# Attention, routed experts and a bilinear network in one kernel: bias constants built first on GpSimd, the mask folded into the distance, and idle products on TensorE

## The chip, the cores and the metric

The kernel runs on one core of a Trainium2 chip. The metric is the device time of one execution in microseconds (us). The two kernels differ in a few small instructions, in their order, and in products whose result nobody reads; the output is the same array.

## What is computed

Three stages follow each other. Attention over q, k, v of shape (4, 8, 576, 64), in a causal window of 128 with a slope per head on the distance:

```python
rel = pos[:, None] - pos[None, :]
slopes = 2.0 ** (-8.0 * (np.arange(H) + 1) / H)
mask = (rel >= 0) & (rel < 128)
scores = np.where(mask, scale * q @ k.T + slopes * -np.abs(rel), -1e9)
x = softmax(scores) @ v                      # then 2304 tokens of 512
e = argmax(x @ w_gate + modality_bias[modality_id])      # one of 8 experts
x = prob[e] * (relu(x @ w1[e]) @ w2[e])      # 512 -> 1024 -> 512
out = ((x @ m_w1) * (x @ m_w2)) @ m_w3 @ m_wout          # m_*: 64-bit weights
```

## The kernel before, in words

Large products are made of three products of two-part numbers (a high part and a rest): `mm3` at L290 to L292, and six half-height products per pair of heads in `scores` at L387. `split` (L273 on ScalarE, L275 or L277 on VectorE) makes the two parts. In the first nine chunks `split_pe` lets TensorE subtract the high part with a scaled identity, `id_k` or `id_q` (L283, L284, L287).

**Attention.** Queries come in chunks of 128 per batch (four and a tail of 64). A unit is a chunk and a half of its heads, 40 units in all. A unit passes through `scores` (TensorE), `softmax` (VectorE adds `bias` to the scores and takes the minimum, L415; ScalarE does the exponential, L420), `p_transposes` (L440) one unit later and `attend` (L459) two units later. Scores are negated, so the mask is a large positive bias. The transposes of the next chunk (L307) and its loads (L166, on the SyncE queue) stand between the units. Also between them, from unit 5 on, the 64-bit weights are loaded (`raw_wo`, `raw_w`, L697) and turned into 32-bit numbers on VectorE (`to_f32`, L710 to L723), and `m_w3 @ m_wout` is built up in the PSUM tile `pw` of tag "G".

**Constants.** `build_constants` makes on GpSimd the identity (L187, L188), the distance `rel` and a separate mask `msk` (L195 to L203: an iota, a cast, a memset, four selections), then on VectorE `bias` of 8 heads as distance times slope plus mask (L209), and after that the smaller constants: `ones_b`, `tri_b`, the zeros of `qz` (L221). `build_constants2` (called at unit 2: gate weights, ten small loads, `mid_f`, and L254 to L266 on VectorE) and `build_constants3` (at unit 3) follow.

**Experts.** Tokens are gathered by expert in blocks of 480 (`gather_x`, L980), transposed in four parts of 120 (`block_transposes`, L1001), and run through `ffn_step`: products `ph` and `py`. Five blocks are in the program in any case. At the **border** to the last network the outputs go through memory: `ys` is written, `load_y` reads it (L1183), `x2_split` makes its two parts, `w_late` (L1133) has eight leftover products on TensorE, and then `ab_step` (products `p`) and `out_step` (products `po`) run to the end.

**Order.** Each engine runs its own list in order. The lists are laid out ahead of time from the program's order and from simulated times; `with tc.issue_after(x)` keeps the instructions of the block behind x in the list of x's engine, and does no more than that. SyncE issues nearly all loads in one list.

Of the kernel before, what the change touches and what calls it, by code (L numbers as in the profile page):

```python
# [18 lines left out]
P = 128  # L19
# [29 lines left out]
def kernel(  # L49
# [134 lines left out]
    def build_constants():  # L184
        scr = a_p.tile([P, 3, 2 * P], F32, tag="p", name="scr", bufs=2)
        rel_i, rel, msk = scr[:, 0, :].bitcast(I32), scr[:, 1, :], scr[:, 2, :]
        nc.gpsimd.memset(ident, 0.0)  # L187
        nc.gpsimd.affine_select(  # L188
            out=ident, in_=ident, pattern=[[-1, P]], compare_op=ALU.not_equal, fill=1.0,
            base=0, channel_multiplier=1,  # L190
        )
        for t, f in ((id_k, -1.0), (id_q, 1.0 / SCALE)):
            nc.vector.tensor_scalar_mul(t, ident, f)

        nc.gpsimd.iota(rel_i, pattern=[[-1, 2 * P]], base=P, channel_multiplier=1)  # L195
        nc.gpsimd.tensor_copy(rel, rel_i)
        nc.gpsimd.memset(msk, 0.0)
        for t, fill in ((rel, 0.0), (msk, MASK)):
            nc.gpsimd.affine_select(
                out=t, in_=t, pattern=[[-1, 2 * P]], compare_op=ALU.is_ge, fill=fill,  # L200
                base=P, channel_multiplier=1,
            )
            nc.gpsimd.affine_select(  # L203
                out=t, in_=t, pattern=[[1, 2 * P]], compare_op=ALU.is_ge, fill=fill,
                base=-1, channel_multiplier=-1,
            )
        for h in range(H):
            slope = 2.0 ** (-8.0 * (h + 1) / H)
            nc.vector.scalar_tensor_tensor(  # L209
                out=bias[:, h, :], in0=rel, scalar=slope, in1=msk, op0=ALU.mult, op1=ALU.add  # L210
            )
# [12 lines left out]
        nc.gpsimd.tensor_copy(iota_em, ie)  # L224
# [44 lines left out]
    last = {}  # L269

    def split(hi, lo, src, scale=1.0):

# [8 lines left out]
    def split_pe(hi, lo, tp, scale=1.0):  # L281

        nc.scalar.activation(out=hi, in_=tp, func=AF.Copy, scale=scale)  # L283
        nc.tensor.matmul(  # L284
            tp, lhsT=id_q if scale != 1.0 else id_k, rhs=hi, start=False, stop=True, skip_group_check=True,
# [3 lines left out]
    def mm3(dst, lh, ll, rh, rl, start, stop):  # L289
        nc.tensor.matmul(dst, lhsT=lh, rhs=rh, start=start, stop=False)  # L290
        nc.tensor.matmul(dst, lhsT=lh, rhs=rl, start=False, stop=False)  # L291
        return nc.tensor.matmul(dst, lhsT=ll, rhs=rh, start=False, stop=stop)  # L292

# [10 lines left out]
    def head_transposes(nm, b, c, tp, hps):  # L304
        t = raw[nm, b, c]
        for hp in hps:
            nc.tensor.matmul(  # L307
                tp[:, hp, :],
# [64 lines left out]
    def scores(b, c, hq):  # L373
# [6 lines left out]
        for t in range(2):  # L380
            hp = 2 * hq + t
            if c < NF:
                for i, (l, r) in enumerate(((ql, kh), (qh, kl), (qh, kh))):

                    for j in (1, 0):
                        d = slice(j * D, (j + 1) * D)
                        last["s"] = nc.tensor.matmul(  # L387
                            s[j][:, t, :nk], lhsT=l[d, hp, :], rhs=r[d, hp, ks],
# [43 lines left out]
    def p_transposes(b, c, hq):  # L432
# [3 lines left out]
        for j in range(2 if c < NF else 1):  # L436
            pt = pst("P", [P, 2, 2, P], f"PT_{b}_{c}_{hq}_{j}")
            for t in range(2):
                for kb in range(nkb):
                    nc.tensor.transpose(pt[:, t, kb, :], p[:, j, t, kb * P : (kb + 1) * P], ident)  # L440
            nc.scalar.copy(pT[:, j, :, :nkb, :], pt[:, :, :nkb, :])  # L441
        st_T[b, c, hq] = pT

    def attend(b, c, hq):
# [6 lines left out]
        for t in range(2):  # L451
            hp = 2 * hq + t
            for i, (kb, cc) in enumerate(kbs):
                for j in (1, 0):
                    if c < NF:
                        pj = pT[:, j, t, kb, :]
                    else:
                        pj = pT[:, 0, t, kb, j * TAIL : (j + 1) * TAIL]
                    nc.tensor.matmul(  # L459
                        av[j * D : (j + 1) * D, hp, : P if c < NF else TAIL],  # L460
# [26 lines left out]
    def gate_logits(i, g, pos):  # L487
# [5 lines left out]
        for d in range(ND):  # L493
            nc.tensor.transpose(
                tp[:, 2 * d : 2 * d + 2, :].rearrange("p h d -> p (h d)"), xt[:, d, :], ident
            )
        lp = pst("A", [P, H, E], f"lg_{i}")
        if i in rs:

            r = rs.pop(i)  # L500
            for d in range(ND):
                nc.tensor.matmul(
                    lp[:, 2 * d : 2 * d + 2, :], lhsT=xt[:, d, :], rhs=wgb[:, d, :, :],
# [13 lines left out]
        else:  # L517
            for d in range(ND):
                nc.tensor.matmul(
                    lp[:, 0, :], lhsT=xt[:, d, :], rhs=wg[:, d, :],  # L520
# [9 lines left out]
    def route(g, i0, m):  # L530
# [30 lines left out]
        for j in range(i0, i0 + m):  # L561
# [3 lines left out]
        rk = pst("A", [P, 6, E], f"rk_{g}")  # L565
        nc.tensor.matmul(
            rk[:, :m, :], lhsT=tri_b, rhs=hot_b[:, sl, :], start=True, stop=False
        )
        nc.tensor.matmul(
            rk[:, :m, :], lhsT=ones_b, rhs=hcum[:, sl, :], start=False, stop=True  # L570
# [21 lines left out]
    def block_table():  # L592
# [6 lines left out]
        np_ = pst("A", [P, 6, E], "cnt")  # L599
        nc.tensor.matmul(np_[:, 0, :], lhsT=ones_b, rhs=hcum[:, NT, :], start=True, stop=True)  # L600

# [151 lines left out]
    def w3_transposes(i, sp=split):  # L753
# [4 lines left out]
        for j in range(4):  # L758
            nc.tensor.matmul(
                tp[:, j, :], lhsT=x[:, j * P : (j + 1) * P], rhs=ident, is_transpose=True,  # L760
# [79 lines left out]
    load_chunk(*chunks[1], "v")  # L840
    extras = {2: [build_constants2], 3: [build_constants3], 5: [fill_rest]}
# [151 lines left out]
    def block_transposes(b, u):  # L993
# [6 lines left out]
        for d in range(ND):  # L1000
            nc.tensor.transpose(tp[:, d, :RU], xb[b][u][:RU, d * P : (d + 1) * P], ident[:RU, :RU])  # L1001
        us = slice(u * RU, (u + 1) * RU)
# [126 lines left out]
    def w_late(f, k):  # L1129

        tag, bufs = (("S", 2), ("P", 2), ("G", 1), ("V", 1), ("S", 2), ("P", 2))[k % 6]
        late[f] = pst(tag, [P, DM], f"pl_{f}", bufs=bufs)
        nc.tensor.matmul(late[f], lhsT=w3_last[:, f, :], rhs=wo_last, start=True, stop=True)  # L1133

# [116 lines left out]
    for f in range(LATE, NMC):  # L1251
        w_late(f, f - LATE + 2)
    for h in range(M_PRE):
        split_m(h)
# [66 lines left out]
```

## Time and profile before

| | us |
|---|---|
| runs of the kernel before | 793.8, 801.9, 802.56 |
| median | 801.9 |
| the profiled execution | 802.81 |
| its span, first to last instruction | 801.1 |
| around the span | 1.7 |
| TensorE busy | 761.4 (95%) |
| VectorE busy | 392.7 (49%) |
| ScalarE busy | 326.6 (41%) |
| GpSimd busy | 70.1 (9%) |

The span holds attention up to about 245 us, the experts up to about 485 us and the last network from 495 us on. TensorE's busy time is modelled and covers all of the pipelined products, so 95% does not say that it runs at its best rate. The mean granted clock of TensorE is 0.979 of full speed.

### The profile page before, as it was taken

What the parts mean: (1) busy time and instruction counts of PE and PEld (TensorE: products, weight loads), DVE (VectorE), ACT (ScalarE), POOL (GpSimd) and SP (SyncE); (2) the same over time, 40 slices, a digit from 0 to 9 for tenths busy, and PEclk for the clock granted to TensorE, in tenths of its full rate; (3) what the DMA queues carried; (4) which work ended last, traced back from release to release, by engine and by line L of the source; (5) the groups of instructions that cost most, each with busy time, mean ns of one, the idle gap of its engine ahead of it and who ended that gap; (6) DMA issues with size and microseconds to landing.
All of it is one profiled execution on the core that took longest, in us unless ns stands there. A gap on an engine that the chain in (4) does not pass through costs nothing. (4 is left out here: it accounts for less than half of the span.)

```text
span 801.1 us, 11805 instructions
## 1 busy us (share of the span) xinstructions
PE 761.4 (95%) x4363; PEld 631.6 (79%) x4363; DVE 392.7 (49%) x1045; ACT 326.6 (41%) x757; POOL 70.1 (9%) x113
## 2 busy tenths in 40 slices
PE   7788999998998899999999997999999999999996
PEld 5676777786776788888888884888888888888895
DVE  4799678685655466566667515541122123023020
ACT  5788677675553334343424313442222122122121
POOL 4000201001013200010100000001000000100101
PEclk9999999998999999999999998999999999999999
DMA  7677645453102958484745204002002000100100
GB/s 154 204 212 204 155 120 148 117 145 81 53 28 68 284 169 265 136 249 138 220 160 165 79 1 130 29 0 79 27 0 79 27 1 27 53 1 0 40 14 27
DMA packets 100502, 81.92 MB, mean 102 GB/s; under 512 B 69850, under 2 KB 83418, under 8 KB 100437
## 3 DMA queue, kind: packets, MB, share of 16 engines
q1 hardware_dynamic: 93925, 66.52, 29.5%
q0 software_dynamic: 3632, 9.66, 3.6%
q10 hardware_dynamic: 2880, 4.92, 1.6%
q8 instruction: 36, 0.59, 0.3%
q14 instruction: 29, 0.24, 0.1%
HBM read 66.36 MB, written 14.54 MB: 101 GB/s over the span
## 5 line engine op out<-in xcount | busy, mean ns | idle before, releaser
L1214 DVE TENSOR_TENSOR a<-a,p 128x512 f32<-128x512 f32 (+1 forms) x40 | 25.4, 634 | 189.7 <-PE p L292 183.5
L275 DVE TENSOR_TENSOR fwl<-fw,fwh 128x1024 fp32r<-128x1024 f32 x40 | 49.0, 1225 | 77.3 <-ACT fwh L273 75.7
L273 ACT ACTIVATE fwh<-fw 128x1024 fp32r<-128x1024 f32 x40 | 42.4, 1061 | 92.4 <-PE ph L291 66.9
L420 ACT ACTIVATE p<-p,mn 128x256 f32<-128x256 f32 (+2 forms) x144 | 68.0, 476 | 27.1 <-DVE mn L415 25.4
L290 PE MATMUL ph<-xbh,fwh 128*128 128x480 f32 x160 | 62.1, 389 | 0.7 <-ACT xbh L273 0.7
L290 PE MATMUL p<-x2h,m0h 128*128 128x512 f32 (+1 forms) x160 | 59.5, 372 | 3.2 <-ACT x2h L273 3.2
L292 PE MATMUL ph<-xbh,fwl 128*128 128x480 f32 x160 | 61.4, 384 | 0.0
L291 PE MATMUL ph<-xbl,fwh 128*128 128x480 f32 x160 | 61.2, 382 | 0.0
L291 PE MATMUL py<-hl,fwh 128*128 128x480 f32 x160 | 60.4, 381 | 0.0
L290 PE MATMUL p<-x2h,m1h 128*128 128x512 f32 (+1 forms) x160 | 59.4, 374 | 0.0
L291 PE MATMUL p<-x2l,m1h 128*128 128x512 f32 (+1 forms) x160 | 59.3, 371 | 0.0
L292 PE MATMUL p<-x2h,m1l 128*128 128x512 f32 (+1 forms) x160 | 59.3, 371 | 0.0
L291 PE MATMUL p<-x2l,m0h 128*128 128x512 f32 (+1 forms) x160 | 59.1, 369 | 0.0
L292 PE MATMUL p<-x2h,m0l 128*128 128x512 f32 (+1 forms) x160 | 59.1, 369 | 0.0
L273 ACT ACTIVATE abh<-a 128x512 fp32r<-128x512 f32 (+1 forms) x40 | 23.5, 588 | 84.6 <-DVE a L1214 84.6
L292 PE MATMUL py<-hh,fwl 128*128 128x480 f32 x160 | 57.9, 380 | 0.0
L290 PE MATMUL py<-hh,fwh 128*128 128x480 f32 x160 | 57.6, 379 | 0.0
L291 PE MATMUL po<-Wl,abh 128*128 128x512 f32 (+1 forms) x152 | 57.3, 378 | 0.0
L290 PE MATMUL po<-Wh,abh 128*128 128x512 f32 (+1 forms) x152 | 57.3, 378 | 0.0
L292 PE MATMUL po<-Wh,abl 128*128 128x512 f32 (+1 forms) x152 | 56.8, 378 | 0.0
L415 DVE CUSTOM_DVE_ANT_0 p<-S,bias 128x256 f32<-128x256 f32 (+1 forms) x128 | 43.4, 386 | 15.5 <-PE S L387 8.9
L459 PE MATMUL av<-pT,vr 128*64 128x128 f32 (+1 forms) x576 | 45.2, 275 | 1.4 <-ACT pT L441 1.1
(231 smaller groups left out, 1616.8 us busy)
## 6 DMA issues: line engine op xcount, KB each, us to landing
fw<-in_moe_w_dram SPq DMA_DIRECT2D x40, 512.0 KB, 4.2
raw_w<-in_moe_w_dram SPq DMA_DIRECT2D x16, 512.0 KB, 4.2
raw_m<-in_moe_w_dram SPq DMA_DIRECT2D x16, 512.0 KB, 3.7
ys_dram<-y ACTq DMA_DIRECT2D x20, 240.0 KB, 4.5
vr<-in_v_dram SPq DMA_DIRECT2D x16, 256.0 KB, 3.7
raw_wo<-in_moe_w_out_dram SPq DMA_DIRECT2D x8, 512.0 KB
xs_dram<-x SPq DMA_DIRECT2D x16, 256.0 KB
yt<-ys_dram SPq DMA_DIRECT2D x8, 512.0 KB, 4.3
```

The costliest lines, as they stand in the source:

```text
L273: last["a"] = nc.scalar.activation(out=hi, in_=src, func=AF.Copy, scale=scale)
L275: last["v"] = nc.vector.tensor_tensor(out=lo, in0=src, in1=f32(hi), op=ALU.subtract)
L290: nc.tensor.matmul(dst, lhsT=lh, rhs=rh, start=start, stop=False)
L291: nc.tensor.matmul(dst, lhsT=lh, rhs=rl, start=False, stop=False)
L292: return nc.tensor.matmul(dst, lhsT=ll, rhs=rh, start=False, stop=stop)
L415: nc.vector.tensor_tensor_reduce(out=p[:, j, t, :nk], in0=s[j][:, t, :nk], in1=bi, scale=1.0, scalar=BIG, op0=ALU.add, op1=ALU.min, accum_ ...
L420: nc.scalar.activation(out=p[:, j, t, :nk], in_=p[:, j, t, :nk], func=AF.Exp, scale=-1.0, bias=m1, accum_out=sm[:, col : col + 1],)
L459: nc.tensor.matmul(av[j * D : (j + 1) * D, hp, : P if c < NF else TAIL], lhsT=raw["v", b, cc][:, 2 * hp + j, :], rhs=pj, start=(i == 0), s ...
L1214: nc.vector.tensor_tensor(out=a[:, :nt], in0=a[:, :nt], in1=pp[1][:, :nt], op=ALU.mult)
```

## The change

In `build_constants` the order on GpSimd becomes identity, iota, cast, two selections, and nothing else. The selections write a far distance, 1e9 times 2^8, outside of the window, so that every head's slope (2^-1 to 2^-8) leaves at least 1e9 there; the mask's memset, its two selections and the tile `msk` go. `bias` is then one scaled copy per head (`tensor_scalar_mul`) instead of `scalar_tensor_tensor` with two inputs. The memset of `ones_b` goes to VectorE, ahead of everything. The rest of the constants (`build_constants1`, and the GpSimd part of `build_constants2` and `3`) stays behind the last of the two selections (`p_mark`) in GpSimd's list.

Idle products, `ones_b` by `ones_b` of 128x512 in bfloat16 into a PSUM tile that nobody reads, are added on TensorE: 5 before the first load has landed, 1 behind the first transposes, 2 behind the scores of each of the units 0 to 4, 2 behind the second half of chunk 0's transposes, 2 behind the transposes of chunks 1 and 2 (22 in the head); 3 behind each of the four parts of the first block's transposes (12); and 16 at the border behind the last of the `w_late` products. Except for the first 5 they are kept behind the TensorE instruction that the program issued last.

```diff
 def build_constants():
-    nc.gpsimd.memset(msk, 0.0)
-    for t, fill in ((rel, 0.0), (msk, MASK)):
-        nc.gpsimd.affine_select(out=t, in_=t, pattern=[[-1, 2 * P]], compare_op=ALU.is_ge, fill=fill,
-            base=P, channel_multiplier=1)
-        nc.gpsimd.affine_select(out=t, in_=t, pattern=[[1, 2 * P]], compare_op=ALU.is_ge, fill=fill,
-            base=-1, channel_multiplier=-1)
+    nc.vector.memset(ones_b, 1.0)
+    far = MASK * 2.0**8
+    nc.gpsimd.affine_select(out=rel, in_=rel, pattern=[[-1, 2 * P]],
+        compare_op=ALU.is_ge, fill=far, base=P, channel_multiplier=1)
+    mark = nc.gpsimd.affine_select(out=rel, in_=rel, pattern=[[1, 2 * P]],
+        compare_op=ALU.is_ge, fill=far, base=-1, channel_multiplier=-1)
     for h in range(H):
-        nc.vector.scalar_tensor_tensor(
-            out=bias[:, h, :], in0=rel, scalar=slope, in1=msk, op0=ALU.mult, op1=ALU.add)
-    nc.gpsimd.memset(ones_b, 1.0)
+        nc.vector.tensor_scalar_mul(bias[:, h, :], rel, 2.0 ** (-8.0 * (h + 1) / H))
+    return mark
+
+def build_constants1():
     nc.gpsimd.memset(tri_b, 1.0)
...
+def idle_work(n, tag="A", bufs=2, first=False):
+    t = pst(tag, [P, 4, P], "idle", bufs=bufs)
+    with nullcontext() if first else tc.issue_after(last["pe"].ins):
+        for _ in range(n):
+            nc.tensor.matmul(t, lhsT=ones_b, rhs=ones_b.unsqueeze(1).to_broadcast([P, 4, P]),
+                start=True, stop=True)
...
-build_constants()
+p_mark = build_constants()
+with tc.issue_after(p_mark.ins):
+    build_constants1()
+idle_work(5, "G", 1, first=True)
...
 transposes_k(*chunks[0], halves[0][1])
+idle_work(1, "G", 1)
...
     if i < nu:
         scores(*units[i])
+        if i < 5:
+            idle_work(2, "G", 1)
         softmax(*units[i])
     if i == 0:
         with tc.issue_after(last["s"].ins):
             transposes_q(*chunks[0], halves[1][1])
             transposes_k(*chunks[0], halves[1][1])
+        idle_work(2, "G", 1)
...
             with tc.issue_after(last["s"].ins):
                 transposes(*chunks[ci])
+            if i < 4:
+                idle_work(2, "G", 1)
...
             for u in range(NU):
                 block_transposes(b0, u)
+                idle_work(3, "S", 2)
...
 for f in range(LATE, NMC):
     w_late(f, f - LATE + 2)
+idle_work(16)
 for h in range(M_PRE):
     split_m(h)
```

The matmul calls of the rest of the kernel go through `pe` and `pe_t`, which only note the last one.

## Rows read from the trace of the kernel before

**Rows 1.** Stretches: busy us (count) of each engine, granted clock, DMA share, GB/s.

```profile
24.30:28.20 3.90, 0.00 (x0) 0.00 (x0) 2.92 (x12) 2.06 (x7) 0.00 (x0) 1.00 0.98 294
28.20:33.20 5.00, 4.95 (x32) 4.46 (x32) 4.97 (x17) 5.00 (x15) 0.00 (x0) 0.66 0.49 139
33.20:60.00 26.80, 24.73 (x225) 19.76 (x224) 25.44 (x83) 20.63 (x58) 0.41 (x2) 1.00 0.71 195
60.00:93.00 33.00, 30.24 (x263) 24.13 (x263) 31.41 (x127) 24.29 (x77) 4.27 (x4) 1.00 0.75 198
192.10:203.20 11.10, 11.03 (x59) 8.91 (x60) 5.47 (x22) 5.87 (x19) 0.00 (x0) 0.55 0.35 75
265.10:268.20 3.10, 3.08 (x8) 2.53 (x9) 1.88 (x2) 1.85 (x2) 0.00 (x0) 0.50 0.79 241
491.90:495.10 3.20, 0.00 (x0) 0.01 (x1) 3.20 (x6) 2.91 (x7) 0.00 (x0) 0.77 0.96 319
495.10:500.40 5.30, 5.28 (x13) 4.14 (x14) 4.48 (x8) 1.59 (x3) 0.00 (x0) 0.50 0.25 75
```

**Rows 2.** Timeline of VectorE in the head: start, duration, [idle before <- releaser].

```profile
1.94 1.77 DVE L193 TENSOR_SCALAR id_k<-ident 128x128 fp32r<-128x128 f32 x1 [1.94 <-POOL ident L188]
...
8.27 2.79 DVE L209 SCALAR_TENSOR_TENSOR bias<-scr 128x256 f32<-128x256 f32 x8 [4.49 <-POOL scr L203]
10.98 0.28 DVE L415 CUSTOM_DVE_ANT_0 p<-S,bias 128x128 f32<-128x128 f32 x1
...
17.63 0.46 DVE L254 TENSOR_SCALAR inv<-mid_f 128x18 f32<-128x18 f32 x1 [2.78 <-POOL mid_f L250]
...
25.28 0.43 DVE L710 TENSOR_SCALAR w_wo<-raw_wo 128x512 int32<-128x512 int32 x1 [5.12 <-DMA raw_wo<-in_moe_w_out_dram]
...
30.53 0.42 DVE L415 CUSTOM_DVE_ANT_0 p<-S,bias 128x256 f32<-128x256 f32 x1
```

**Rows 3.** Timeline of GpSimd in the head.

```profile
2.19 1.44 POOL L221 MEMSET qz<- 128x512 f32 x3
...
7.84 0.40 POOL L203 TENSOR_SCALAR_AFFINE_SELECT scr<-scr 128x256 f32<-128x256 f32 x1
```

**Rows 4.** Timeline of TensorE's products (PE) in the head.

```profile
3.36 0.66 PE L307 MATMUL qtp<-ident,qr 128*128 128x128 f32 x2 [3.36 <-DMA qr<-in_q_dram]
...
7.25 0.42 PE L387 MATMUL S<-kTh,qTh 64*128 64x128 f32 x2
```

**Rows 5.** Timeline of TensorE's weight loads (PEld) in the head.

```profile
4.49 0.29 PEld L284 LDWEIGHTS qtp<-qTh,id_q 128*128 128x128 f32 x1
...
21.25 0.19 PEld L284 LDWEIGHTS ktp<-kTh,id_k 128*128 128x128 f32 x1
```

**Rows 6.** Groups on VectorE, 12 to 60 us: count, busy us, mean ns.

```profile
L415 DVE CUSTOM_DVE_ANT_0 p<-S,bias 128x256 f32<-128x256 f32 x24 | 8.9, 420 | 0.2 <-PE S L387 0.2
...
L710 DVE TENSOR_SCALAR w_wo<-raw_wo 128x512 int32<-128x512 int32 x6 | 2.5, 414 | 5.1 <-DMA raw_wo<-in_moe_w_out_dram 5.1
```

**Rows 7.** Timeline of TensorE at the first block of the experts.

```profile
263.87 0.60 PE L1001 MATMUL btp<-ident,xb 120*128 120x120 f32 x4 [1.16 <-DMA xb<-xs_dram,ids]
265.12 1.17 PE L290 MATMUL ph<-xbh,fwh 128*128 128x480 f32 x2 [0.66 <-ACT xbh L273]
```

**Rows 8.** Timeline of the border.

```profile
490.77 1.13 PE L1133 MATMUL pl<-wo_last,w_last 128*128 128x512 f32 x2 [0.71 <-DVEq L1154]
...
494.39 1.15 ACT L273 ACTIVATE x2h<-yt 128x512 fp32r<-128x512 f32 x2 [0.29 <-DMA yt<-ys_dram]
...
495.21 2.65 DVE L275 TENSOR_TENSOR x2l<-yt,x2h 128x512 fp32r<-128x512 f32 x4
```

**Rows 9.** The chain that ended last: start, length, piece (products of 512 columns).

```profile
498.02 0.43 PE p L291
...
502.64 0.23 PE p L291
```

**Rows 10.** Waits of VectorE, 100 to 265 us: us in total, times, longest.

```profile
DVE p L415 <- remote: 2.8, 1, 2.8
```

More of the change, by code (lines that the diff above doesn't have):

```diff
@@ L1 @@
-from contextlib import ExitStack
+from contextlib import ExitStack, nullcontext
 import concourse.bass as bass
@@ L184, in build_constants @@
     def build_constants():
-        scr = a_p.tile([P, 3, 2 * P], F32, tag="p", name="scr", bufs=2)
-        rel_i, rel, msk = scr[:, 0, :].bitcast(I32), scr[:, 1, :], scr[:, 2, :]
+        scr = a_p.tile([P, 2, 2 * P], F32, tag="p", name="scr", bufs=2)
+        rel_i, rel = scr[:, 0, :].bitcast(I32), scr[:, 1, :]
+        nc.vector.memset(ones_b, 1.0)
         nc.gpsimd.memset(ident, 0.0)
@@ L191, in build_constants @@
         )
+        nc.gpsimd.iota(rel_i, pattern=[[-1, 2 * P]], base=P, channel_multiplier=1)
         for t, f in ((id_k, -1.0), (id_q, 1.0 / SCALE)):
             nc.vector.tensor_scalar_mul(t, ident, f)
-        nc.gpsimd.iota(rel_i, pattern=[[-1, 2 * P]], base=P, channel_multiplier=1)
         nc.gpsimd.tensor_copy(rel, rel_i)
-        nc.gpsimd.memset(msk, 0.0)
-        for t, fill in ((rel, 0.0), (msk, MASK)):
[L199 to L206, printed above, removed]
-        for h in range(H):
-            slope = 2.0 ** (-8.0 * (h + 1) / H)
-            nc.vector.scalar_tensor_tensor(
-                out=bias[:, h, :], in0=rel, scalar=slope, in1=msk, op0=ALU.mult, op1=ALU.add
-            )
-        nc.gpsimd.memset(ones_b, 1.0)
+        far = MASK * 2.0**8
+        nc.gpsimd.affine_select(
+            out=rel, in_=rel, pattern=[[-1, 2 * P]], compare_op=ALU.is_ge, fill=far,
+            base=P, channel_multiplier=1,
+        )
+        mark = nc.gpsimd.affine_select(
+            out=rel, in_=rel, pattern=[[1, 2 * P]], compare_op=ALU.is_ge, fill=far,
+            base=-1, channel_multiplier=-1,
+        )
+        for h in range(H):
+            nc.vector.tensor_scalar_mul(bias[:, h, :], rel, 2.0 ** (-8.0 * (h + 1) / H))
+        return mark
+    def build_constants1():
         nc.gpsimd.memset(tri_b, 1.0)
@@ L269, with pe, pe_t @@
     last = {}
+    def pe(*args, **kw):
+        last["pe"] = nc.tensor.matmul(*args, **kw)
+        return last["pe"]
+    def pe_t(*args):
+        last["pe"] = nc.tensor.transpose(*args)
+    def idle_work(n, tag="A", bufs=2, first=False):
+        t = pst(tag, [P, 4, P], "idle", bufs=bufs)
+        with nullcontext() if first else tc.issue_after(last["pe"].ins):
+            for _ in range(n):
+                nc.tensor.matmul(
+                    t, lhsT=ones_b, rhs=ones_b.unsqueeze(1).to_broadcast([P, 4, P]),
+                    start=True, stop=True,
+                )
     def split(hi, lo, src, scale=1.0):
@@ L289, in mm3 @@
     def mm3(dst, lh, ll, rh, rl, start, stop):
-        nc.tensor.matmul(dst, lhsT=lh, rhs=rh, start=start, stop=False)
-        nc.tensor.matmul(dst, lhsT=lh, rhs=rl, start=False, stop=False)
-        return nc.tensor.matmul(dst, lhsT=ll, rhs=rh, start=False, stop=stop)
+        pe(dst, lhsT=lh, rhs=rh, start=start, stop=False)
+        pe(dst, lhsT=lh, rhs=rl, start=False, stop=False)
+        return pe(dst, lhsT=ll, rhs=rh, start=False, stop=stop)
     NP = H // 2
@@ L306, in head_transposes @@
         for hp in hps:
-            nc.tensor.matmul(
+            pe(
                 tp[:, hp, :],
@@ L386, in scores @@
                         d = slice(j * D, (j + 1) * D)
-                        last["s"] = nc.tensor.matmul(
+                        last["s"] = pe(
                             s[j][:, t, :nk], lhsT=l[d, hp, :], rhs=r[d, hp, ks],
@@ L599, in block_table @@
         np_ = pst("A", [P, 6, E], "cnt")
-        nc.tensor.matmul(np_[:, 0, :], lhsT=ones_b, rhs=hcum[:, NT, :], start=True, stop=True)
+        pe(np_[:, 0, :], lhsT=ones_b, rhs=hcum[:, NT, :], start=True, stop=True)
         fe, f0 = t("fe", E), t("f0", 1)
@@ L840, with const2, const3 @@
     load_chunk(*chunks[1], "v")
-    extras = {2: [build_constants2], 3: [build_constants3], 5: [fill_rest]}
+    def const2():
+        with tc.issue_after(p_mark.ins):
+            build_constants2()
+    def const3():
+        with tc.issue_after(p_mark.ins):
+            build_constants3()
+    extras = {2: [const2], 3: [const3], 5: [fill_rest]}
     transposes_q(*chunks[0], halves[0][1])
     transposes_k(*chunks[0], halves[0][1])
+    idle_work(1, "G", 1)
     groups = GROUPS
@@ L1132, in w_late @@
         late[f] = pst(tag, [P, DM], f"pl_{f}", bufs=bufs)
-        nc.tensor.matmul(late[f], lhsT=w3_last[:, f, :], rhs=wo_last, start=True, stop=True)
+        pe(late[f], lhsT=w3_last[:, f, :], rhs=wo_last, start=True, stop=True)
     def w_add(f):
```

20 lines of the change are left out of this document (10 added, 10 removed).

## The prediction

> **What bounds the kernel now.** I read the granted clock and the busy times by stretch first [rows 1], then the timelines of the places where the clock is low or an engine stands still. From 265 us on TensorE has no pause except at the border, so there the end moves by what TensorE gains. Before that there are two regimes. From 28.2 to 93 us VectorE is the bound: it is busy 4.97 of 5.0, 25.4 of 26.8 and 31.4 of 33.0 us [rows 1]; whatever lets it start that stretch earlier moves the stretch. From 93 to 245 us no engine is full, and the units follow each other by latency; a shift that arrives there goes through if the order holds.
>
> The head is what feeds VectorE. Four waits of it matter [rows 2]: bias is made from 8.27 to 11.06 us, so the first softmax begins at 10.98, while the scores of that unit end at 7.25 + 0.42 = 7.67 [rows 4]; bias waited for a selection on GpSimd that ended at 8.24 [rows 3]. Then VectorE stands 2.78 us until `mid_f` at 17.63 and 5.12 us until the first 64-bit weights at 25.28. Both of these end with a DMA, and not with bias.
>
> The low clock shows in stretches with 0.50 (1.2 GHz): 265.1 to 268.2 and 495.1 to 500.4, in part 28.2 to 33.2 and 192.1 to 203.2 [rows 1]. A product of 512 columns then takes 0.43 us against 0.23 [rows 9]. The head's first weight load takes 0.29 us against 0.19 for the same form at 21.25 [rows 5], so its start is at the low level too.
>
> **The change, part by part.**
>
> *Border: -2.3 us.* The last `w_late` product has two passes from 490.77; at 0.43 per pass its last column is in at about 491.7 (estimate from the start and the 1.13 us of the row, which has the way out in it) [rows 8, 9]. Then TensorE does nothing until 495.1, and the clock falls in that gap: 0.77 in it, 0.50 behind it [rows 1]. The 5.26 us from 495.12 to 500.38 hold 5.26 / 0.43 = 12.2 products; at 0.23 they take 2.8, a gain of 2.45. The 16 idle products are in front of them in TensorE's list. The trace has no bfloat16 product of this size; the nearest row is the 512-column product of 0.23 us, and at the low level 0.43 [rows 9], so 16 of them take 3.7 to 6.9 us. I take 0.23, since the clock is at 1.00 up to the gap: they end at 491.7 + 3.7 = 495.4, about 0.2 later than 495.12, when the first real product could go. That is the whole cover: the 3.4 us wait for the DMA and ScalarE's `x2h` at 494.39 [rows 8]. What is late next is VectorE's `x2l`, the last of four at 497.86 [rows 8], against a faster 13th product at 495.4 + 2.8 = 498.2, so it is just in time. Net 2.25, as 2.3; the bounds are -2.5 and, with the idle products at 0.43, 491.7 + 6.9 = 498.6, behind which the 12.2 products take 2.8 and end at 501.4: +1.0.
>
> *First block: -1.3 us.* Between the four parts TensorE waits for gathered tokens and for ScalarE, the last times 1.16 and 0.66 us [rows 7]. Three idle products of 0.23 take 0.69 behind each part. Behind the last they end at 264.47 + 0.69 = 265.16 against 265.12, so they cost nothing; the earlier ones delay the nine `pw` products that stand between the parts, and the third part by some 0.5 us, which the 1.16 us wait for the fourth part's gather takes up. If the clock stays up, 3.0 us at a level of 0.5 (265.1 to 268.2) take 1.5 to 1.65; the eight records of 480 columns in that stretch [rows 1] at 0.23 x 480/512 = 0.215 take 1.7, so the gain is 3.1 - 1.7 = 1.4, less 0.1. The second step's weights are then needed after the first step's 24 products, at 265.1 + 24 x 0.215 = 270.3; ScalarE and VectorE, which split them, are busy 1.85 and 1.88 of the 3.1 us [rows 1] and have room for it. Bounds: -1.4, and +0.6 if each set of three takes 1.3 (the last ends at 265.75).
>
> *Constants.* On GpSimd the chain to bias becomes six instructions (memset, selection, iota, cast, two selections). At 0.40 to 0.48 each (a selection; a third of the three memsets of 1.44) [rows 3] from about 0.8 us on, they end at 3.2 to 3.7 us instead of 8.24. The mask's memset and two selections go. The other constants, `qz` among them, move behind the chain and have no early reader: the first user of `qz` or of `tri_b` is tens of microseconds off. VectorE's eight copies are not in the trace as such. The nearest rows are the eight of L209 in 2.79 us [rows 2], and L710 with one input, 0.41 us for twice the columns [rows 6], so between 8 x 0.21 = 1.7 and 2.8 us; I take the first, as the kind is the same. Bias is there by 3.5 + 1.7 = 5.2, at the latest by 3.7 + 2.8 = 6.5, before the scores. So the first softmax waits for the scores, about 7.0 with a faster clock: 4 us earlier. The memset of `ones_b` on VectorE is below 0.2 us and ahead of any reader.
>
> The two DMA waits decide how much of the 4 us is left. The small loads of `build_constants2` and the weight loads stand in SyncE's list, which `p_mark` does not hold, so `mid_f` and `raw_wo` land about when they do now. Everything that VectorE can finish before 25.28 is a gain, and from there it is full. In the trace unit 3 (four additions of 0.37 = 1.5 us) comes behind the first conversion at 25.28, and unit 4 at 30.53 [rows 2, 6]. If units run 3 to 4 us earlier, both can come before the wait: 2 x 1.4 = 2.8 us. This is my value; the bounds are 0 (nothing crosses the wait) and 4 (all of it).
>
> *Idle products of the head: +0.5 us.* Five of 0.43 from about 1.0 end at 3.2, before the first load at 3.36 [rows 4]: free. The other 17 take 3.9 us at 0.23 and 7.3 at 0.43. In 24.3 to 28.2 TensorE has nothing at all to do [rows 1], and before that it mostly waits for ScalarE and VectorE; I count one pair (0.46) on the path, with bounds 0 and 3. That they hold the clock in 28.2 to 33.2 is worth nothing, as VectorE is full there [rows 1].
>
> **Sum** against the profiled execution: 802.8 - 2.3 - 1.3 - 2.8 + 0.5 = 796.9. That execution lies 0.9 above the median of the runs, 801.9, so 796.0 for a median. About 1% of the time, 8 us, is what can be told from no change.
>
> **The rivals.**
>
> *The head's gain is hidden: 798.3.* VectorE comes to the two DMA waits earlier and stands there longer, with the planned order as it is. For it: both waits end with a DMA [rows 2]. Against: their order in the list was planned with a late bias, and may now put the ready units first. Only border and block are left, 802.8 - 3.6 - 0.9 = 798.3, and 0.5 of idle products has cover in longer waits. A second way to the same time is in the copies themselves: id_k, one input, 128 columns, took 1.77 us where L710 takes 0.41 for four times as much; meanwhile GpSimd ran memsets back to back from 2.19 to 3.63 [rows 2, 3, 6]. If the eight copies of bias stand behind the memsets and the rest of GpSimd's list in this way, bias comes at 8 to 10 us. The Trainium skill has a rule for it ("SBUF — State Buffer", Who interferes with whom): `tensor_scalar` can use VectorE's second port, which GpSimd shares, and the one that comes second is blocked for the whole instruction, while the two-input form that is replaced only meets GpSimd's reads. By that rule the change makes the copies worse; the 1.77 us agrees with it. Chance of both ways together: 0.25.
>
> *It doesn't do what it says: 799.* The lists are planned, and the idle products have only a lower bound of place; put elsewhere, they leave the clock as it is, and only the head gains (802.8 - 2.8 - 0.9 = 799.1). Chance 0.07.
>
> *A stall goes too: 788.* At 187.8 VectorE waits 2.8 us, once, for something the trace can't name [rows 10], TensorE stands still, and the clock is then low for ten microseconds [rows 1]. Together this is worth about 2.8 + 11.1 x 0.45 = 7.8 us, and the three times before lie at 793.8 and 802: one run in three seems to be without it. With other timing it may stay away: 796.0 - 8 = 788. For it speaks that the wait has no cause in the data; against it, that the stretch itself is not changed. Chance 0.25.
>
> *Slower: 804.* The idle products run at 0.43 us, since the clock falls in spite of them: border +1.0, block +0.6, and in the head 17 x 0.43 = 7.3 us, of which the 3.9 us pause before 28.2 covers at most 3.9; +3.4 against bias's -2.8. 802.8 + 2.2 - 0.9 = 804.1. It decides from the point at which 16 of them take more than the 3.4 us gap plus the 2.45 they win, 0.37 us each. Against it: the clock was at 1.00 until 491.9 through gaps of about 1 us. Chance 0.08.
>
> **How the numbers follow.** The forecast has 0.35, the others 0.25, 0.07, 0.25 and 0.08. The forecast's own range is 793 to 799 (head 0 to -4 with the rest as counted, and 1 us to either side for a new order). For 8 in 10 the range goes from 787, which takes in most of the case without the stall, to 803. Faster by over 1% means below 793.9: the stall's case and a third of the forecast's lower side, 0.25 + 0.13 = 0.38; slower by over 1% is above 809.9, 0.06 for a new order that goes badly; the rest, 0.56, is within 1%.
>
> **What would show it.** Right: the copies of bias end before 6.5 us and the first L415 starts near 7; no low clock in 265 to 268 and behind the border, with the first `p` product within 0.3 us of `x2h`'s end; VectorE full from about 25.3 with the L415 of units 3 and 4 before the first L710. Wrong: copies of bias of more than 1 us each, L254 and the first L710 in the same place with as much waiting in front as bias has gained, idle products spaced by 0.43 at the border, or a stretch between 93 and 245 us that gives the shift back.

## The result and the profile after

The changed kernel took 789.78, 789.79, 790.36 and 791.54 us, a median of 790.08. The kernel before, run beside it, took 793.8 to 802.56, a median of 800.08. The ratio is 0.9895 with an interval of 0.9848 to 0.9942. The profiled execution of after is the one of 791.54 (span 789.5, mean granted clock 0.988); its 11.6 us are set against the profiled execution of before (span 801.1). How much of this the change can claim is the subject of the experiments: when the two kernels were run again, more often (e7 below), the ratio was 0.9951 (0.9913 to 0.9990).

The windows of after: busy us (count) of PE, PEld, VectorE, ScalarE, GpSimd, then the granted clock, the DMA share and GB/s. The first two are the stretches of [rows 1]; the others follow the shifted work.

```profile
24.30:28.20 3.90, 3.05 (x26) 2.05 (x27) 3.46 (x9) 3.71 (x9) 0.00 (x0) 1.00 0.97 269
28.20:33.20 5.00, 5.00 (x54) 3.89 (x50) 4.78 (x16) 2.32 (x8) 0.00 (x0) 1.00 0.88 242
33.20:57.50 24.30, 21.25 (x192) 16.96 (x188) 22.38 (x76) 19.97 (x59) 0.64 (x2) 1.00 0.70 189
57.50:67.80 10.30, 8.12 (x46) 7.15 (x47) 10.30 (x35) 3.93 (x12) 0.00 (x0) 0.50 0.64 183
182.90:196.60 13.70, 13.12 (x118) 10.36 (x117) 10.15 (x43) 11.39 (x38) 3.84 (x4) 1.00 0.35 60
257.00:260.50 3.50, 3.49 (x16) 2.68 (x16) 3.16 (x4) 2.97 (x4) 0.34 (x1) 1.00 0.75 234
486.00:491.20 5.20, 5.17 (x23) 4.21 (x24) 4.34 (x7) 1.60 (x3) 0.00 (x0) 1.00 0.25 66
```

The empty stretch of TensorE at 24.3 is filled, and the clock is whole at 28.2, at the scatters (182.9), at the first block (257) and behind the border (486). Between 33.2 and 57.5 VectorE stands 1.9 us (1.4 in the 26.8 us from 33.2 to 60 in [rows 1]), 1.8 of them in one wait that is shown further down. A new low stretch of 10.3 us follows from 57.5; VectorE is busy through all of it.

VectorE's timeline in the head of after, for [rows 2]: start, duration, in brackets the idle time before and its releaser.

```profile
1.69 0.40 DVE L196 TENSOR_SCALAR id_k<-ident 128x128 fp32r<-128x128 f32 x1 [0.61 <-POOL ident L189]
...
2.98 2.15 DVE L209 TENSOR_SCALAR bias<-scr 128x256 f32<-128x256 f32 x1 [0.76 <-POOL scr L204]
5.05 1.74 DVE L209 TENSOR_SCALAR bias<-scr 128x256 f32<-128x256 f32 x7
7.73 0.29 DVE L432 CUSTOM_DVE_ANT_0 p<-S,bias 128x128 f32<-128x128 f32 x1 [0.94 <-PE S L272]
...
15.27 0.29 DVE L432 CUSTOM_DVE_ANT_0 p<-S,bias 128x128 f32<-128x128 f32 x1 [6.60 <-PE S L272]
...
21.32 0.42 DVE L432 CUSTOM_DVE_ANT_0 p<-S,bias 128x256 f32<-128x256 f32 x1 [0.41 <-PE S L272]
...
24.58 0.43 DVE L727 TENSOR_SCALAR w_wo<-raw_wo 128x512 int32<-128x512 int32 x1 [1.79 <-DMA raw_wo<-in_moe_w_out_dram]
...
31.27 0.42 DVE L432 CUSTOM_DVE_ANT_0 p<-S,bias 128x256 f32<-128x256 f32 x1
```

GpSimd's timeline in after, for [rows 3]: the distance is done 5.3 us earlier, and six memsets (`tri_b`, `hcum` and four of `qz`) now run from 2.89 to 4.99, beside VectorE's first copy, which starts 0.09 us behind the first of them and ends at 5.13.

```profile
2.55 0.40 POOL L204 TENSOR_SCALAR_AFFINE_SELECT scr<-scr 128x256 f32<-128x256 f32 x1
2.89 0.20 POOL L213 MEMSET tri_b<- 128x128 bf16 x1
...
3.08 1.91 POOL L221 MEMSET qz<- 128x512 f32 x4
```

TensorE's timeline in after: the head ([rows 4]), the first block ([rows 7]) and the border ([rows 8]).

```profile
1.13 2.31 PE L283 MATMUL idle<-ones_b 128*128 128x512 bf16 x5 [1.13 <-DVE ones_b L187]
3.34 0.66 PE L272 MATMUL qtp<-ident,qr 128*128 128x128 f32 x2
...
7.28 0.41 PE L272 MATMUL S<-kTh,qTh 64*128 64x128 f32 x2
7.63 1.04 PE L283 MATMUL idle<-ones_b 128*128 128x512 bf16 x2
...
256.24 0.81 PE L283 MATMUL idle<-ones_b 128*128 128x512 bf16 x3
257.07 0.70 PE L272 MATMUL ph<-xbh,fwh 128*128 128x480 f32 x2
...
482.32 3.62 PE L283 MATMUL idle<-ones_b 128*128 128x512 bf16 x16
...
486.03 0.47 PE L272 MATMUL p<-x2h,m0h 128*128 128x512 f32 x1
```

At the head the five idle products take 0.46 each, at the border 16 take 3.62, 0.23 each: the low level and the high one.

Following the same instructions through both timelines gives the place of each gain (after less before, us). `x` is VectorE's write of one tile of 128 tokens at the end of attention (18 tiles); `ph` and `hh` are the first product of the experts and its result, `pl` is a product of `w_late`:

```
first exponential                     -3.4   (11.5 -> 8.1)
x of the first tile                   -5.9   (33.2 -> 27.3)
x of the sixth tile                   +0.7   (97.6 -> 98.3)
x of the thirteenth                   +0.6   (171.7 -> 172.3)
x of the eighteenth                   -6.6   (241.6 -> 235.0)
first product of the experts (ph)     -8.0   (265.1 -> 257.1)
first hh                              -9.3   (269.8 -> 260.5)
last pl, ahead of the border          -9.4   (491.3 -> 481.9)
end                                  -11.6   (801.1 -> 789.5)
```

About 7.2 us come between 172 and 242, where the change has no instruction; 2.7 at the first block, 2.2 at the border.

The head's gain looks as if it were there at 33 us and gone at 97, but the -5.9 of the first `x` is mostly a change of order. VectorE's idle time from the start shows it:

```
up to                          before                       after
the first x                    33.2: busy 17.0, idle 16.2   27.3: busy 13.0, idle 14.3
the fourth x                   61.3: busy 43.7, idle 17.6   59.3: busy 42.9, idle 16.4
the sixth x                    97.6: busy 74.1, idle 23.5   98.3: busy 74.7, idle 23.6
```

At the first `x` after has saved 1.9 us of idle time; the other 4.0 us are work that before has done by then and after still has to do (weight conversions among it). At the sixth `x` both have done the same work, with the same idle time.

### The profile page after: what moved, and what is told of

The parts are those of the page before. It is cut to its first block, busy times and chain, and to the rows that moved or that the text cites. A ratio compares the mean times of both kernels' runs of the same rounds, so it can differ in the third digit from the quotient of the medians.

```text
span 789.5 us, 11893 instructions
## 1 busy us (share of the span) xinstructions
PE 764.3 (97%) x4413; PEld 628.8 (80%) x4413; DVE 393.3 (50%) x1046; ACT 326.6 (41%) x757; POOL 68.8 (9%) x109
## 5 line engine op out<-in xcount | busy, mean ns | idle before, releaser
L290 ACT ACTIVATE abh<-a 128x512 fp32r<-128x512 f32 (+1 forms) x40 | 23.5, 588 | 87.2 <-DVE a L1250 87.2
L272 PE MATMUL py<-hh,fwl 128*128 128x480 f32 x160 | 57.9, 380 | 0.0
L432 DVE CUSTOM_DVE_ANT_0 p<-S,bias 128x256 f32<-128x256 f32 (+1 forms) x128 | 43.0, 387 | 14.5 <-PE S L272 13.6
```

The lines of the kernel that those rows point to most:

```text
L272: last["pe"] = nc.tensor.matmul(*args, **kw)
L290: last["a"] = nc.scalar.activation(out=hi, in_=src, func=AF.Copy, scale=scale)
L432: nc.vector.tensor_tensor_reduce(out=p[:, j, t, :nk], in0=s[j][:, t, :nk], in1=bi, scale=1.0, scalar=BIG, op0=ALU.add, op1=ALU.min, accum_ ...
```

## The experiments

Three sets of four kernels were run, each set on one chip with the kernel before beside it. In all but two cases a kernel has 12 runs; the kernel before has 29, 35 and 29. "Clock" is the mean of the runs' mean granted clocks.

```
            edit                                  median  before   ratio (95%)            clock
set 1 e1    border products alone                 798.43  798.54   0.9989 (0.9953-1.0025) 0.984
      e2    block products alone                  796.55           0.9999 (0.9963-1.0035) 0.984
      e3    new constants alone (6 runs)          804.18           1.0117 (1.0057-1.0176) 0.971
      e4    the head's idle products alone        794.33           0.9963 (0.9926-1.0000) 0.982
set 2 e5    after without the head's products     800.60  797.48   1.0026 (0.9987-1.0066) 0.976
      e6    block and border products             794.42           0.9947 (0.9913-0.9981) 0.989
      e7    after                                 794.21           0.9951 (0.9913-0.9990) 0.984
      e8    after with the old constants          792.99           0.9963 (0.9920-1.0007) 0.982
set 3 e9    e5, conversions one group later       807.69  806.43   1.0004 (0.9975-1.0033) 0.973
      e10   e6 + new mask, GpSimd's order free    801.09           0.9952 (0.9915-0.9990) 0.980
      e11   after + 13 more pairs                 803.23           0.9961 (0.9938-0.9984) 0.983
      e12   after, conversions later (6 runs)     793.18           0.9835 (0.9795-0.9876) 0.983
```

The kernel before took 792.7 to 806.0 within set 1, and its clock was 0.982 in the mean of sets 1 and 2. In these 29 runs time and mean clock go together (correlation -0.92, 6.1 us for each 0.01 of clock); in set 2 it is -0.87 and 5.0. The scatter of this kernel goes mostly with the clock.

### Each part alone

**Border (e1).**

```diff
+    idle_work(16)
     for h in range(M_PRE):
```

> The kernel before with the 16 idle products at the border as its only change; every list is as before up to the border. Theory A (the gain is a sum of places that don't touch each other, of which the border is 2.3 us): the stretch from the first product behind the border on is at the high clock, its first 12 products are spaced by 0.23 instead of 0.43 us, and the kernel ends 2.2 to 2.5 us before the kernel before, once the same attention stage is taken off. Theory B (nearly all of the 10 us come from the head, whose new order keeps a stall in the attention stage away): the same at the border, but under 1 us in the time. The single stall at 188 us of the kernel before should be seen in the profile here too if it belongs to the order of the lists, which is the same.

The whole time can't tell 2.3 us here, but the stretch can. Windows of e1 (the border products alone, the second one is behind the border) and of e4 (none at the border, the second one is behind it):

```profile
28.10:45.20 17.10, 16.54 (x91) 14.85 (x92) 12.26 (x38) 9.87 (x28) 0.00 (x0) 0.50 0.35 104
...
491.80:497.00 5.20, 5.14 (x23) 3.69 (x22) 5.02 (x9) 2.31 (x4) 0.00 (x0) 1.00 0.26 65
```

```profile
484.20:487.60 3.40, 0.93 (x2) 0.10 (x1) 2.78 (x5) 3.14 (x6) 0.00 (x0) 1.00 0.69 208
487.60:494.40 6.80, 5.12 (x12) 4.08 (x13) 5.27 (x9) 2.30 (x4) 0.00 (x0) 0.50 0.34 101
```

With the products 23 of TensorE's instructions fit into 5.2 us behind the gap, without them 12 into 6.8 (5.1 of them busy). All four profiles without the 16 products (before, e2, e3, e4) have the low level there, none of the ten with them. From the last `pl` to the 121st `p` it is 33.6, 34.0, 34.1 and 34.4 us without, and 31.3 to 32.1 with: 2.4 us between the means. From the first `p` to the 121st it is 29.3 to 29.8 without and 27.3 to 27.4 with.

**Block (e2).**

```diff
                     block_transposes(b0, u)
+                    idle_work(3, "S", 2)
```

> The kernel before with only the idle products behind the four parts of the first block's transposes. Theory A: the low clock at 265 to 268 us goes, for 1.2 to 1.4 us; between the end of attention and the first product of the experts nothing changes by more than 0.3 us, since what shortened that stretch by 1.5 us in the changed kernel is the gather, not the idle products. If the 1.5 us are theirs too, the gain is 2.5 to 3 us. Theory B: under 0.5 us.

From the first `ph` to the first `hh` it is 4.7 us in before, 3.4 in after, 3.7 in e2. But e1, e3 and e4, which have no block products either, show 3.4 to 3.5, and no low clock there (and e5, which has them, 4.9, at a whole clock). The low stretch at 265 of [rows 1] is in one profile of the four without the products. So the 1.3 us is a price that before's profiled run happened to pay, not one that the products save in every run. The time agrees with the second theory: 0.9999.

**Constants (e3).** The diff of `build_constants` and `p_mark` alone.

> Only the constants of the change: the chain to bias first on GpSimd, the mask in the distance, scaled copies on VectorE; no idle product. First softmax near 7.5 us. Theory A (the head's start is given back before 90 us): the time stays within 2 us of the kernel before with the same attention stage, and the units at 90 to 180 us come within 1 us of where they were. Theory B (the head is what gains): 5 to 8 us faster. A third view: the idle products of the head are what gives the start back, then this one keeps 2 to 4 us of it at 90 us.

First exponential at 7.6 us, and yet 1.2% slower. The sixth `x` comes at 102.0, beside 103.4 and 102.2 in e1 and e2 with the old constants: little of the earlier start is left. Windows of e3, then its waits from 44 to 62 us on VectorE and on TensorE (total, times, longest):

```profile
50.20:60.40 10.20, 10.20 (x58) 9.61 (x58) 8.55 (x31) 7.13 (x22) 0.41 (x2) 0.50 0.33 95
67.20:70.60 3.40, 3.40 (x17) 3.40 (x18) 3.40 (x13) 1.78 (x3) 0.00 (x0) 0.51 0.85 255
```

```profile
DVE w_wo L727 <- DMA raw_wo<-in_moe_w_out_dram: 1.7, 1, 1.7
```

```profile
PE S L272 <- DVE mn L432: 1.7, 1, 1.7
```

A conversion waits for its load, TensorE for the softmax behind it, and at 50 us the clock falls for 10 us. The runs' mean clock is 0.971 against 0.982, which by the slope above goes with 6 us; the medians differ by 5.6. That the wait brings the clock down is not shown: in after and in e7, two profiles of one program, the clock falls at 57.5 and 57.9 us, and the wait for a load ahead of it is 1.8 us in the one and 0.3 in the other.

**The head's idle products (e4).**

```diff
+    idle_work(5, "G", 1, first=True)
...
+            if i < 5:
+                idle_work(2, "G", 1)
...
+                if i < 4:
+                    idle_work(2, "G", 1)
```

> Only the 22 idle products of the head (and the memset of their operand on VectorE, which they need); constants as before. If idle products raise the clock in the head, the low stretches at 15.7 to 19.3 and 28.2 to 33.2 us go and the first rise comes before 12.3 us; from the changed kernel I expect the first rise not to move and the later two stretches to go. Theory A: no gain or up to 2 us slower, since VectorE waits for bias and two DMAs as before and TensorE has more to do. Theory B: 1 to 3 us faster.

The first rise of the clock is at 13.2 and the two low stretches are gone, as was expected from the changed kernel. The first exponential is later here (15.2 against 11.5), and the median is still 4.2 us lower; the interval of the ratio reaches 1.0000. The reason that rows suggest: e1, e2 and e6 have before's instructions in before's order in the head (e6's window is the one below) and lose 4.6 to 5.8 us between 28 and 50 us, because the clock is low there for 13 to 17 us; before's own profile was low for 3.4 only [rows 1]. In e4 it is whole from 13.2 to 50.7. In the low stretch VectorE waits for the others: from 26 to 50 us it stands 2.9 us for scores and 3.2 for an exponential in e6, and 0.2 and 1.0 in before, which has the same list.

```profile
28.30:45.40 17.10, 16.67 (x91) 14.97 (x92) 12.13 (x38) 9.88 (x28) 0.00 (x0) 0.50 0.38 108
```

### What the parts do together

> The changed kernel without the 22 idle products of the head (5 before the first products, and those behind the first groups); new constants, block and border products stay. Theory A (the 11 us are the clock's: the head's idle products keep the low stretches short between 15 and 45 us, and new constants by themselves only move the wait): about 798 to 801, 1.0% or more over the changed kernel, with low stretches at 16 to 19 and 28 to 45 us in its profile. Theory B (the new constants carry the gain of the head, the idle products there are ornament): within 0.4% of the changed kernel, 788 to 793.

> The kernel before with the idle products at the block transposes and at the border, and nothing of the head. Theory A: the border gives 2.3, the block 0 to 1.3, the scatter from run to run (10 us and more) stays since it comes from the attention stage: median 794 to 798 beside 798 to 800 for the kernel before. Theory B' (block and border together carry most of the 11 us): 790 or less with little scatter.

> The changed kernel once more, so that the others of this set stand beside it on the same chip. All theories: 789 to 792 with a scatter under 4 us. If its scatter is as wide here as that of the kernel before (10 us and more), the first comparison was luck in part and the gain is about the 3 to 5 us of border, block and constants.

> The changed kernel with the old constants (mask apart, eight two-input adds, built in the old order; only the memset of the ones stays first on VectorE, since the idle products read it); all idle products stay. Theory A (the constants add nothing of their own once the head's idle products hold the clock): within 0.3% of the changed kernel, 789 to 793, although its first exponential comes about 7 us later (15 us beside 8). Theory B (the constants carry a gain of their own, that needs the idle products beside it): 793 to 796, 0.4 to 0.8% over the changed kernel.

e6 and e7 have the same median, 794.4 and 794.2: block and border alone reach what after gains over before in this set. Of the 3 us, 2.4 are seen in the rows of the border; the rest is within the scatter. Without the head's products the new constants cost 6.2 us (e5 over e6), and the head's products give 6.4 back (e7 under e5). e5's time is that of theory A, its low stretches are not (29.2 to 32.6 and 49.7 to 59.9 us). With the old constants the head's products bring -1.4 in the median and +1.0 in the mean (e8 against e6), which is nothing that twelve runs can tell. After's 789 to 792 with under 4 us of scatter did not come: it took 789.4 to 802.1 here. The narrow four runs of the first comparison were in part luck, as the third expectation had allowed for.

The two halves of the constants come apart in e10, which has the mask in the distance but leaves GpSimd's order free (the rule is dropped for `build_constants2` and `3` too).

```diff
-    with tc.issue_after(p_mark.ins):
-        build_constants1()
+    build_constants1()
```

> The kernel before with block and border products and the mask in the distance, but without the rule that the other constants come behind the distance on GpSimd (the smaller half of the constants edit); no idle products in the head. VectorE's list then has the second softmax of chunk 1 ahead of the first conversions again. Theory C: 794 to 797, as with the old constants (794.4). Rival (the earlier start itself, or the eight copies, lose the time): 799 to 802, as with the whole constants edit (800.6).

0.9952 against 0.9947 for e6, though on two chips: the new mask costs nothing and gains nothing that the runs can tell. By the number alone, 801.1 us, the rival would be right, but before stands at 806.4 on this chip, and the ratio is what can be compared. So the loss of e5 goes with the rule of order (`p_mark`): on e10's own chip e9, which has the rule and later conversions, takes 6.6 us more. The rows show where it may begin. With the rule VectorE's additions of unit 3 (L432) stand behind the first conversion, which waits for its load (e5, the first timeline), and without the rule ahead of it (e10, the second):

```profile
23.10 0.43 DVE L727 TENSOR_SCALAR w_wo<-raw_wo 128x512 int32<-128x512 int32 x1 [1.33 <-DMA raw_wo<-in_moe_w_out_dram]
...
26.25 0.42 DVE L432 CUSTOM_DVE_ANT_0 p<-S,bias 128x256 f32<-128x256 f32 x1
```

```profile
22.61 0.42 DVE L432 CUSTOM_DVE_ANT_0 p<-S,bias 128x256 f32<-128x256 f32 x1 [1.06 <-PE S L272]
...
25.11 0.43 DVE L727 TENSOR_SCALAR w_wo<-raw_wo 128x512 int32<-128x512 int32 x1 [1.04 <-DMA raw_wo<-in_moe_w_out_dram]
```

Up to the sixth `x` VectorE is idle for 25.8 us in e5 and 23.1 in e10. That is 2.7 of the 6 us; the rest is not followed. VectorE's timeline of e10 also prices the copies:

```profile
1.69 2.09 DVE L196 TENSOR_SCALAR id_k<-ident 128x128 fp32r<-128x128 f32 x1 [0.62 <-POOL ident L189]
...
7.36 1.71 DVE L209 TENSOR_SCALAR bias<-scr 128x256 f32<-128x256 f32 x8 [3.51 <-POOL scr L204]
```

With GpSimd idle beside them the eight copies take 1.71 us, 0.21 each. In after the first of them starts at 2.98, in the memset of `tri_b`, stands through that one and the five memsets behind it, and takes 2.15; the other seven take 1.74. `id_k` goes the other way: 2.09 beside the memsets in e10, 0.40 in after ahead of them.

### Trying to take the wait away

e9 (on e5) and e12 (on after) convert both weights one group later and load them as before:

```diff
-LEAD = [4, 3, 1]
+LEAD = [4, 2, 1]
...
-        at(WO_AT[g], lambda g=g: split_wout(g))
+        at(WO_AT[g] + 1, lambda g=g: split_wout(g))
```

> New constants, block and border products, no idle products in the head (as the run without the head's idle products, 800.6 us median), and the conversions of the two weights one group later in the written order, their loads where they were. Theory C (with the new constants the conversions stand ahead of a softmax on VectorE and wait 1.3 to 1.9 us for their loads at 23 and 45 us; TensorE then waits 1.7 us for the softmax, and the clock falls behind it at 50 us): the waits for raw_wo go, no low stretch from 50 to 60, median 794 to 797, mean granted clock 0.985 or more. Rival D (the loss is the head's clock alone, drawn anew in every run): waits gone or not, median 799 to 802, mean clock 0.975.

> The changed kernel with the conversions of the two weights one group later, their loads where they were. Theory C: no wait for raw_wo or raw_w from 23 to 60, the low stretch at 57 to 68 gone or shorter, median 789 to 792 with few runs over 795 (the changed kernel here: 794.2, half of its runs over 795). Rival D: as the changed kernel, 793 to 795 with the same scatter. Rival F (later weights make the first weight products late): 796 or more with a new wait of TensorE for woh or w3h.

Theory C's remedy failed in e9: the waits for `raw_wo` are still there (3.3 us, two of them), the clock is low at 17, 30, 51 and 65 us, the time is that of before. In e12 the wait is even longer (4.1 us), the low stretch from 58.4 to 68.7 is as in after, and the sixth `x` begins at 98.6 (after 98.3). Yet e12 is the fastest kernel against its neighbours, 1.65% under before. Where a good part of that comes from is told under the stall, below.

> The changed kernel with the pair of idle products behind the first 18 groups in place of the first 5 (13 more pairs, up to about 70 us). Theory E (the pairs hold the clock wherever they stand): no low stretch from 48 to 69, mean clock 0.990 or more, median 789 to 791. Rival (TensorE is 85 to 97% busy there, so that the pairs come on top: 13 x 0.6 = 7.8 us less what falls into gaps): 795 to 800 at a mean clock of 0.990.

```diff
-            if i < 5:
+            if i < 18:
```

Theory E fell: e11 is still low at 39.0, 49.2 and 62.9 us, for 3.4 each time, and stands to before as e6 does. The rival's clock of 0.990 did not come either (0.983). e11's runs are close together (801.7 to 805.4), but 13 more pairs did not bring the time down.

### The stall at the scatters

VectorE's waits from 183 to 196 us in e10, for [rows 10], which show the same wait in before:

```profile
DVE p L432 <- remote: 2.9, 1, 2.9
```

Windows of e10, the stretch behind it:

```profile
193.90:204.10 10.20, 10.20 (x50) 8.50 (x50) 3.45 (x19) 4.83 (x15) 0.00 (x0) 0.50 0.22 75
```

e9 and e11 show both as well, e12 neither (its clock is whole from 183 to 196). TensorE's products of that place had ended by their records up to 3.3 us before the semaphore events that report them (187.34, the event at 190.61 in before). Since the recorded ends of products are modelled, this does not tell whether the products or the events were late. GpSimd runs its four scatters at that moment. From the thirteenth `x` to the eighteenth the four profiles with the stall take 69.9 to 70.9 us, the ten without 62.2 to 63.1: it costs 7 to 8 us. On set 3's chip before was at 806.4 in place of 798, and three of the four kernels there show the stall; in sets 1 and 2 none of eight does. e1, e2 and e6 have before's lists up to there and do not stall, e11 has every part of the change and does, e12 has them with later conversions and does not. So the stall does not belong to the order of the lists, and no part of the change takes it away by itself. What decides (the chip, the moment at which the scatters meet TensorE's products) is open: the scatters and the late events coincide in time, and that one holds up the other is not shown.

## Why the prediction was right or wrong

The four runs of the first comparison, 789.8 to 791.5, lie in the wide range of 787 to 803 and below the forecast's own range of 793 to 799. The border came as forecast, the first block in size only, and the head's gain was all but gone at the sixth `x`. What brought the time down further is the missing stall, which the prediction had as a rival and the range had taken in, and which no part of the change brings about by itself. So the time is in the range in good part by luck.

**Border, -2.3: right in size and cause.** The 16 products took 3.62 us (3.7 was forecast), ended at 485.9, and the first `p` started at 486.03; the low stretch is gone in ten profiles of ten. 2.2 to 2.4 us.

**First block, -1.3: the size fits, the cause does not hold.** The clock at the block is whole in after, but also in three kernels without the products. The step that failed is the first one: one profile's low stretch was taken as the kernel's own. The remaining 1.4 us of the block's 2.7 lie before `ph`; from VectorE's first `row_i` (the row numbers of the blocks) to `ph` it is 18.9 to 20.5 us, with 19.7 in the mean of the kernels with the products and 19.9 without, so it is scatter of that stretch, and not the products' doing.

**Constants, -2.8: the step that failed.** The chain on GpSimd was sized too high: it ended at about 2.95 against 3.2 to 3.7. The copies were outside their bounds: from 2.98 to 6.79 it is 3.81 us where 1.7 to 2.8 were given. The value of 0.21 each was right (e10), but the first copy stood 1.9 us longer, until the six memsets were through. That is what the second way of the first rival described, `id_k`'s 1.77 us of [rows 2] over again, though not with its size: it had bias at 8 to 10 us. The Trainium skill ("SBUF — State Buffer", Who interferes with whom) has the engine that comes second to the shared port blocked for the whole instruction of the other. The copy came second, 0.09 us behind the memset of `tri_b`, which agrees with it; that it was held through six memsets in a row is more than the one instruction that it speaks of.

Bias at 6.79 was still ahead of the scores, and the first softmax came at 7.73, 3.25 us earlier. Unit 3 did go ahead of the first conversion (21.32), unit 4 did not (31.27). Then the text said that VectorE is full from 25.3 on and carries the gain, 2.8 us for two units that cross the wait. One unit crossed, and VectorE's idle time was 1.9 us less at the first `x`; at the sixth it was the same (23.5 and 23.6 us). VectorE stood 1.8 us at 55.3 for `raw_w`, and TensorE behind it for 2.2. That wait is the first rival's mechanism, met 30 us later than where it was put. The low stretch behind it takes nothing more from VectorE, which is busy for all of its 10.30 us.

The wait is not all of it. In e7, a second profile of the same program, it is 0.3 us; the clock falls at 57.9 all the same, and the sixth `x` comes at 96.6, 1.0 us ahead of before. So the head's gain at that point is between -0.7 and 1.0 us in two profiles, at the lower end of the 0 to 4 that the prediction gave, or just below it.

VectorE's and TensorE's longest waits in after from 44 to 62 us:

```profile
DVE w_w L727 <- DMA raw_w<-in_moe_w_dram: 1.8, 1, 1.8
```

```profile
PE lg L272 <- DVE x L523: 2.2, 1, 2.2
```

The same two waits in e7:

```profile
DVE w_w L727 <- DMA raw_w<-in_moe_w_dram: 0.3, 1, 0.3
```

```profile
PE lg L272 <- DVE x L523: 0.7, 1, 0.7
```

**Idle products of the head, +0.5: the price can't be told, the worth was missed.** Unit 1 begins at 15.27 in after and at 13.27 in before, but also at 15.39 in e5 without them, and at 12.76 in e8 with them. "That they hold the clock in 28.2 to 33.2 is worth nothing, as VectorE is full there" is wrong for the runs in which the clock is low for 13 to 17 us there: in e1's window above VectorE is busy 12.26 of 17.1 us, TensorE 16.54. That the products keep such stretches away is seen in the profiles (none of the six with them is low from 28 to 38 us, seven of the eight without are); what it is worth in time is not settled: 0.9963 with an interval up to 1.0000 in e4, nothing to be told in e8, and 6.4 us beside `p_mark` (e7 under e5).

**The stall.** 7.2 us of the 11.6 come from its absence; 7.8 was forecast, at a chance of 0.25, and as something that other timing may bring. That the run of 793.8 was one without the stall is not shown: e1 and e2, with before's lists up to there, took 797.9 and 800.9 in profiles without it. The profile of after is the stall's rival with the head's gain hidden: -2.3, -2.7, +0.6 and -7.2. In set 2, where none of the four profiles shows the stall (before was not profiled there), the ratio is 0.9951, 3.3 us in the medians; the forecast was 796.0 against 801.9, 5.9 us.

**Slower** did not happen; its condition, idle products at 0.43 at the border, did not either.

e12 is the version to try next: 0.9835 of before, against 0.9952 and 0.9961 for e10 and e11 on the same chip. It was not run beside after, and a good part of its lead is the missing stall.

## What to carry to other kernels

Before a low stretch of clock or a nameless wait of one profile is counted as a gain, see whether it is in a second profile of the same program: here identical instruction lists differed by 6 us in one stretch and 7 in another. Idle products pay where an engine's pause is fixed from outside, as at the border, and they fit into it at the high level. Where a chain of loads sets the pace, work done earlier may only wait at the next load. A start that moved is no gain yet: the first `x` came 5.9 us earlier, and 4.0 of that was work put behind it; compare the idle time of the engine up to the same amount of work. A part that loses alone can be repaired by another part of the same change, so take each alone and take each out.

## What was not expected of the hardware

- The first rise of the granted clock came at 4.2 to 13.5 us in the six profiles that begin with five products of 512 columns back to back from 1.13 us (13.15 in after, 13.2 in e4, 4.2 in e8), and at 12.3 to 22.4 in the eight that do not. The same list gave 12.3 in before and 20 to 21.5 in e1, e2 and e6.
- A one-input copy of 128x256 on VectorE took 0.21 us with GpSimd idle and 2.15 beside six memsets of GpSimd in a row (2.89 to 4.99 us); a 128x128 copy took 0.40 ahead of them and 2.09 beside them.
- TensorE's semaphore events came up to 3.3 us behind the recorded (modelled) ends of its products, in four profiles of fourteen, while GpSimd ran the same four scatters.
